# Hash attention and gated feed-forward: the normed rows of five half batches turned by DMA instead of TensorE

## The chip, the cores and the metric

The kernel runs on one core of one Trainium2 chip. The metric is the device time of one execution in microseconds; lower is better. Before the change three runs took 341.55, 342.83 and 345.98 us, so the median is 342.83 us.

## What is computed

Attention with hash buckets: a query sees only the keys whose six sign bits agree with its own. Its result, heads side by side, goes row by row through a root-mean-square norm and a gated feed-forward layer.

```python
# q, k, v: (4, 8, 768, 64); proj: (64, 6)
q_bits = einsum('bhsd,dk->bhsk', q, proj) > 0      # k_bits likewise
mask = bucket(q_bits)[:, :, :, None] == bucket(k_bits)[:, :, None, :]
scores = where(mask, q @ k.T / 8, -1e9)
attn = softmax(scores) @ v                         # denominator + 1e-9
x = attn.transpose(0, 2, 1, 3).reshape(3072, 512)
xn = x / sqrt(mean(x * x, -1) + 1e-6) * rms_g
g, val = xn @ w_gate, xn @ w_val                   # 512 -> 1536
out = (g * sigmoid(g) * val) @ w_out               # 1536 -> 512
```

## The kernel before

A batch has 768 tokens. The work is cut into eight half batches w = 0 to 7 of 384 tokens each; w // 2 is the batch. A token row of the feed-forward layer has 512 values, and a half batch has three chunks of 128 tokens.

**Slots.** One slot is a third of one head of one half batch: two score products (`scores`, L329) into a PSUM tile, one exponential over 128x768 (`probs`, L339). There are 192 slots (L34 to L36); from slot 48 on a half batch takes 24 slots. All other work is put into a plan by hand: `at(slot, function, ..., rank=)` (L556) hangs a step on a slot, and the loop at L679 writes the slot's steps out in order of rank: those with a rank below 3 ahead of the exponential, the others behind it, and steps of one rank in the order in which they were hung. The order in which instructions are written is the order in which each engine, and each engine's DMA queue, works them off. So a step that waits holds up what is written behind it on its engine.

**Stages of one half batch w.** `end` (L657) is three slots behind the last slot of a head.

- `av` (L341): the attention weights times v, at slots end-1 and end. Its keys' sums come from `v_sum` and `v_mean`.
- `attn_out` (L355), every second head, at slot end: VectorE adds the constant part (L366) and takes reciprocals (L371); GpSimd multiplies into `x` (L375) and squares (L387).
- `sumsq` (L390), six slots later: VectorE adds the squares of two heads up.
- `norm` (L396): VectorE adds the four parts (L398); GpSimd computes `ms` and, as a power of -0.5, `rstd` (L400, L404).
- `scale_x` (L406), one per chunk: VectorE multiplies the rows by `rstd`, from fp32 to fp16, into `xn` (L409).
- `turn_x` (L411), one per chunk: TensorE transposes the chunk's four 128x128 blocks into one PSUM bank (L416), and VectorE takes the bank into `xnT`, times the gain by column, `gcol` (L417). The feed-forward products need the 512 features on the partitions, and `xnT` has them so: four groups of 128 features by 384 tokens.
- `gate` and `value` (L422, L433), for twelve groups of 128 hidden features over 16 slots, beginning at slot s0 = 24 w + 48: each four matmuls over `xnT`. ScalarE takes a tanh of the gate (L430); VectorE forms `a` and `ht` from it (L440, L441).
- `project` (L447), nine steps over slots s0+16 to s0+24: TensorE multiplies with `wo`, ScalarE copies the bank to `ysb` (L459, two buffers), and SyncE stores it (L461).

For w >= 2 the last head's `end` is 24 w + 26, so the feed-forward part of a half batch runs while the scores of the half batch after next are worked on: gate stage w over slots s0 to s0+16, then its projection stage.

**Banks.** `gps` (L71) has three PSUM banks, in turn for gates, values, turns, projections, hash products and sums; the next user of a bank waits until the one before has been read.

**Loads and hash.** For batches 2 and 3 and the second half of batch 1, `load_blocks` (L115) fetches q and k of a pair of heads in four DMAs each, `load_rows` (L107) v in one, all on SyncE's queue, into a ring of ten raw tiles. VectorE turns q and k in 32x32 blocks (`turn_dve`, L193), GpSimd casts them to fp16 (`cast_pool`, L201), `hash_pairs` (L274) computes the sign bits, and eight (or four) DMAs on SyncE's queue (L288) put them beside q and k. `v_prep` and `v_sum` (L293, L297) cast v and add its six blocks up on GpSimd. The table `work` (L616) holds, per pair of heads (batch, pair), the slots of the k, q and v loads, of the turns, of the casts, and of the hash.

Weights are loaded early by GpSimd's queue. The rows' gain is loaded as `gcol`, 128 partitions by four columns (L551).

```python
    for w in range(8):
        for h in range(H):
            end = LAST[w, h] + 3
```

Of the kernel before, what the change touches and what calls it, by code (L numbers as in the profile page):

```python
# [8 lines left out]
FP32 = mybir.dt.float32  # L9
FP16 = mybir.dt.float16  # L10
AF = mybir.ActivationFunctionType
ALU = mybir.AluOpType
# [5 lines left out]
D = 64  # L18
DMODEL = H * D
# [7 lines left out]
KBIT = -32.0  # L27
ESCALE = 1.0 / 8.0
C0 = 1.0e-9

# [11 lines left out]
def kernel(  # L44
# [12 lines left out]
    nc = tc.nc  # L57
    PSUM = bass.MemoryType.PSUM

    const = ctx.enter_context(tc.tile_pool(name="const", bufs=1))  # L60
# [7 lines left out]
    spool = ctx.enter_context(tc.tile_pool(name="spool", bufs=2))  # L68
# [13 lines left out]
    scl = const.tile([128, 1], FP32, name="scl")  # L82
    mhalf = const.tile([128, 3], FP32, name="mhalf")
    gcol = const.tile([128, 4], FP32, name="gcol")
    wg = const.tile([128, 4, DFF], FP16, name="wg")
    wv = const.tile([128, 4, DFF], FP16, name="wv")
    wo = const.tile([128, NF, DMODEL], FP16, name="wo")
    vls = [const.tile([128, H, 6, 66], FP16, name=f"vl{i}") for i in range(2)]
    vsum = [const.tile([128, H, 66], FP16, name=f"vsum{i}") for i in range(2)]
    cvb = [const.tile([128, H, 66], FP32, name=f"cvb{i}") for i in range(2)]  # L90

    def bank(name, shape=None, dt=FP32):
        return gps.tile(shape or [128, 512], dt, name=name, tag="g")
# [203 lines left out]
    def v_sum(b, hp):  # L297
        vn = raw[b, hp, "v"]
        hs = slice(2 * hp, 2 * hp + 2)
        a = spool.tile([128, 2, 3, D], FP32, name="vadd")  # L300
        nc.gpsimd.tensor_add(a, vn[:, :, 0:3], vn[:, :, 3:6])
        nc.gpsimd.tensor_add(a[:, :, 0], a[:, :, 0], a[:, :, 1])
        nc.gpsimd.tensor_add(vsum[b % 2][:, hs, 0:64], a[:, :, 0], a[:, :, 2])

    def v_mean(b, hp, n, parts=(None,)):
        hs = slice(2 * hp, 2 * hp + n)
        ps = bank("m_ps", [128, n, 65])
        for i, jt in enumerate(parts):
# [3 lines left out]
            )  # L312
        nc.vector.tensor_scalar_mul(cvb[b % 2][:, hs, 0:65], ps, C0 / S)  # L313


    sps, psb, ot = {}, {}, {}
    x, ssp, xn, xnT, ht = {}, {}, {}, {}, {}
# [76 lines left out]
    rstds = {}  # L394
# [11 lines left out]
    def scale_x(w, c):  # L406
        if w not in xn:
            xn[w] = npool.tile([128, 3, DMODEL], FP16, name="xn")
        nc.vector.tensor_scalar_mul(xn[w][:, c, :], x[w][:, c, :], rstds[w][:, c : c + 1])  # L409

    def turn_x(w, c):  # L411
        if w not in xnT:
            xnT[w] = npool.tile([128, 4, HALF], FP16, name="xnT", bufs=2)
        ps = bank("x_ps", [128, 4, 128], FP16)
        for kt in range(4):
            nc.tensor.transpose(ps[:, kt, :], xn[w][:, c, kt * 128 : (kt + 1) * 128], ident16)  # L416
        nc.vector.tensor_mul(  # L417
            xnT[w][:, :, c * 128 : (c + 1) * 128], ps,
            gcol.unsqueeze(2).to_broadcast([128, 4, 128]),
        )  # L420
# [87 lines left out]
    def load_wo(f0, f1):  # L508
        nc.gpsimd.dma_start(
            out=wo[:, f0:f1, :],  # L510
            in_=moe_w_out[f0 * 128 : f1 * 128, :].rearrange("(k p) n -> p k n", p=128),
        )

    def columns_of_proj():
# [41 lines left out]
    def at(s, f, *a, rank=3):  # L556
        plan[s].append((rank, len(plan[s]), lambda: f(*a)))
# [36 lines left out]
    for i, (t, src) in enumerate(((wg, moe_w_gate), (wv, moe_w_val))):  # L594
        at(2 + 4 * i, load_w, t, src, 0, 768)
        at(12 + 5 * i, load_w, t, src, 768, 1536)
        at(33 + 6 * i, load_wo, 6 * i, 6 * i + 6)
# [15 lines left out]
    def in_row(loads, s, hash_slot=None):  # L613
        return loads, range(s, s + 8), (s + 4, s + 8, s + 9), hash_slot
# [2 lines left out]
        (1, 2): ((21, 23, 30), (36, 37, 40, 40, 48, 49, 50, 51), (42, 52, 46), 53),  # L617
        (1, 3): in_row((42, 44, 47), 52, 61),
        (2, 0): in_row((54, 56, 59), 61), (2, 1): in_row((64, 67, 70), 71, 80),
        (2, 2): in_row((73, 76, 79), 81), (2, 3): in_row((82, 85, 88), 91, 100),  # L620
        (3, 0): in_row((94, 98, 102), 106), (3, 1): in_row((104, 108, 112), 116, 125),
        (3, 2): in_row((116, 120, 124), 126), (3, 3): in_row((126, 130, 134), 136, 145),
    }
    for (b, hp), (loads, turns, cast_slots, sh) in work.items():
        for which, s in zip("kqv", loads):
            at(s, load_rows if which == "v" else load_blocks, nc.sync, b, hp, which)
        for i, s in enumerate(turns):
            at(s, turn_dve, b, hp, "kq"[i // 4], i % 4, rank=5)
        for which, s in zip("kq", cast_slots):
            at(s, cast_pool, b, hp, which)  # L630
        if sh:
            at(sh, hash_pairs, b, (hp,) if b == 1 else (hp - 1, hp))
        at(cast_slots[2], v_prep, b, hp)
        at(cast_slots[2], v_sum, b, hp)
        if hp % 2:
            at(64 if b == 1 else 48 * b - 4 + 4 * hp, v_mean, b, hp - 1, 4)
    for hp in range(2):
        at(52 + 4 * hp, v_mean, 1, hp, 2, range(6))

    gts, sqs = {}, {}  # L640

# [13 lines left out]
# [3 lines that stand above are left out]
            at(end - 1, av, w, h, 0, 9)  # L658
            at(end, av, w, h, 9, 18)
            if h % 2:  # L660
                at(end, o_step, w, h // 2, rank=4.5)
                if (w, h) != (0, 7):
                    at(end + 6, s_step, w, h // 2, rank=5)
        at(end + (1 if w == 0 else 9), norm, w, rank=5)
        for c in range(3):
            at(end + (3 if w == 0 else 14 + c), scale_x, w, c, rank=5)
            at(end + (7 + c if w == 0 else 17 + 2 * c), turn_x, w, c, rank=1)
        s0 = 24 * w + 48
        seen = set()
        for ft in range(NF):  # L670
            for f, s in ((g_step, s0 + 16 * ft // NF), (v_step, s0 + (32 * ft + 16) // (2 * NF))):
                at(s, f, w, ft, rank=4 if s in seen else 2)
                seen.add(s)
        for i in range(9 if w < 7 else 6):
            c, j = divmod(i, 3)
            at(s0 + 16 + i, project, w, c, 4 * j, 4 * j + 4, rank=1 if i == 8 else 3)


    for s in range(NS + 48):  # L679
# [3 lines left out]
        n = sum(r < 3 for r, _, _ in todo) if s < NS - 1 else 0  # L683
# [54 lines left out]
```

## Time and profile before

| | before |
|---|---|
| median of three runs | 342.83 us (341.55 to 345.98) |
| the profiled execution | 341.45 us, of which the span 339.7 us |
| granted TensorE clock | 1.00 of full speed |
| TensorE busy | 329.8 us (97% of the span) |
| VectorE busy | 238.5 us (70%) |
| ScalarE busy | 210.0 us (62%) |
| GpSimd busy | 151.5 us (45%) |
| 16 DMA engines, packets of SyncE's queue | 31.5% of their span |
| transposes on TensorE into `x_ps` (L416) | 96, of 218 ns each in flight |
| their evictions on VectorE (L417) | 24, 684 ns each |
| scales on VectorE (L409) | 24, 651 ns each |

The span is the time from the profiled execution's first instruction to its last, and what lies around it is the rest of the device time. In the views below, PE is TensorE's matmuls, PEld its weight loads, DVE VectorE, ACT ScalarE, POOL GpSimd and SPq SyncE's queue. A line names the source line (L438), the tile written and the tiles read. TensorE's matmuls overlap, so the duration of one is longer than what it adds to the stream: the chain of waits shows the latter. The row of digits has 40 equal slices of the span, each digit the busy share in tenths.

### The profile page before, as it was taken

How to read it: one execution, taken by the hardware profiler on the slowest of the kernel's cores; microseconds unless marked ns; L12 is line 12 of the kernel's file. 1: busy time of each engine (PE TensorE's matmuls, PEld its weight loads, DVE VectorE, ACT ScalarE, POOL GpSimd, SP SyncE). 2: the span in 40 equal slices, each digit the busy share in tenths (PEclk: the TensorE clock that was granted, in tenths of full speed). 3: DMA queues.
4: the chain of work that ended last, by engine and by line, in shares of the span. 5: the costliest groups of instructions: out<-in, count | busy, mean ns of one | idle time of the engine just before them, and what ended most of it. 6: DMA issues, size and time to landing. Idle time of an engine off the chain costs nothing.

```text
span 339.7 us, 7799 instructions
## 1 busy us (share of the span) xinstructions
PE 329.8 (97%) x3004; PEld 201.5 (59%) x3004; DVE 238.5 (70%) x529; ACT 210.0 (62%) x328; POOL 151.5 (45%) x224
## 2 busy tenths in 40 slices
PE   8899989999999999999999999999999999999995
PEld 7566656564566565566565665566566665555553
DVE  4769798888758895778668886767436653883860
ACT  3789987666566675657666675567666774322321
POOL 4879878437366576335737385503111311110000
PEclk9999999999999999999999999999999999999999
DMA  7999999744646074418243341100010001002002
GB/s 205 351 220 256 196 186 156 140 66 91 117 131 128 17 139 103 91 28 175 64 101 74 59 98 63 39 13 2 31 64 0 3 23 69 5 0 93 3 0 93
DMA packets 80052, 31.36 MB, mean 92 GB/s; under 512 B 65144, under 2 KB 77072, under 8 KB 80016
## 3 DMA queue, kind: packets, MB, share of 16 engines
q1 hardware_dynamic: 76080, 26.09, 31.5%
q0 software_dynamic: 3712, 4.72, 8.6%
q8 instruction: 23, 0.38, 0.5%
q14 instruction: 13, 0.11, 0.1%
q10 hardware_dynamic: 224, 0.07, 0.1%
HBM read 28.32 MB, written 6.29 MB: 102 GB/s over the span
## 4 chain that ended last, share of the span: by engine, by line
PE 88%; DVE 9%; issue 1%; ACT 1%; DVEq 0%; ACTq 0%
PE v_ps L438 18%; PE y_ps L452 18%; PE g_ps L428 18%; PE s_ps L329 16%; PE o_ps L351 9%; PE d_ps L209 5%; PE x_ps L416 1%; PE t_ps L169 1%; DVE otmp L366 1%; PE z_ps L322 1%; PE y_ps L695 1%; DVE xn L409 1%; DVE ssp L391 1%; PE m_ps L310 1%; DVE QK L270 1%
## 5 line engine op out<-in xcount | busy, mean ns | idle before, releaser
L339 ACT ACTIVATE psb<-s_ps 128x768 f16<-128x768 f32 x192 | 150.8, 809 | 29.1 <-PE s_ps L329 27.9
L329 PE MATMUL s_ps<-QK 76*128 76x384 f16 x384 | 93.5, 325 | 1.3 <-ACT psb L339 0.7
L430 ACT ACTIVATE t<-g_ps 128x384 f32<-128x384 f32 x96 | 47.1, 490 | 62.4 <-PE g_ps L428 62.1
L438 PE MATMUL v_ps<-xnT,wv 128*128 128x384 f16 x384 | 78.0, 325 | 0.9 <-DVE cvb L313 0.5
L428 PE MATMUL g_ps<-xnT,wg 128*128 128x384 f16 x384 | 78.0, 325 | 0.4 <-DVE xnT L417 0.4
L440 DVE SCALAR_TENSOR_TENSOR a<-t,g_ps 128x384 f32<-128x384 f32 x96 | 52.6, 548 | 28.2 <-ACT t L430 26.3
L452 PE MATMUL y_ps<-wo,ht 128*128 128x512 f16 x276 | 69.2, 378 | 0.5 <-DVE a L440 0.5
L375 POOL TENSOR_TENSOR x<-otmp,rcp 128x384 f32<-128x384 f32 x31 | 25.8, 831 | 95.8 <-DVE rcp L371 95.5
L351 PEld LDWEIGHTS <-psb 128*128 128x128 f16 x1152 | 51.5, 97 | 25.0 <-issue 7.5
L441 DVE SCALAR_TENSOR_TENSOR ht<-a,v_ps 128x384 f16<-128x384 f32 x96 | 53.2, 554 | 11.5 <-PE v_ps L438 2.3
L351 PE MATMUL o_ps<-vl,psb 128*128 128x65 f16 x1152 | 56.7, 193 | 0.4 <-DVE otmp L366 0.2
L438 PEld LDWEIGHTS <-wv 128*128 128x128 f16 x384 | 36.3, 97 | 25.3 <-issue 1.7
L428 PEld LDWEIGHTS <-wg 128*128 128x128 f16 x384 | 35.9, 97 | 24.3 <-issue 0.6
L329 PEld LDWEIGHTS <-QK 76*128 76x128 f16 x384 | 31.6, 98 | 16.4 <-issue 3.6
L452 PEld LDWEIGHTS <-ht 128*128 128x128 f16 x276 | 25.8, 97 | 24.3 <-issue 0.6
L459 ACT COPY ysb<-y_ps 128x512 f32<-128x512 f32 x23 | 13.5, 586 | 25.4 <-PE y_ps L452 22.6
L417 DVE TENSOR_TENSOR xnT<-x_ps,gcol 128x512 f16<-128x512 f16 x24 | 16.3, 684 | 15.9 <-PE x_ps L416 15.9
L387 POOL TENSOR_TENSOR sq<-x 128x384 f32<-128x384 f32 x31 | 25.6, 825 | 2.5
L366 DVE TENSOR_TENSOR otmp<-o_ps,cvb 128x390 f32<-128x390 f32 x32 | 17.8, 557 | 10.3 <-PE o_ps L351 10.3
L201 POOL CAST QK<-kT 64x768 f16<-64x768 f32 x20 | 16.7, 834 | 13.5 <-DVE kT L193 6.5
L216 DVE TENSOR_SCALAR bits<-d_ps,thr,scl 128x384 f16<-128x384 f32 (+1 forms) x20 | 13.3, 675 | 11.4 <-PE d_ps L209 10.1
L201 POOL CAST QK<-qT 64x768 f16<-64x768 f32 x20 | 16.7, 835 | 9.2 <-DVE qT L193 8.6
(77 smaller groups left out, 285.9 us busy)
## 6 DMA issues: line engine op xcount, KB each, us to landing
vL<-in_v_dram SPq DMA_DIRECT2D x16, 384.0 KB
out_dram<-ysb SPq DMA_DIRECT2D x23, 256.0 KB
kL<-in_k_dram SPq DMA_DIRECT2D x40, 96.0 KB
qL<-in_q_dram SPq DMA_DIRECT2D x40, 96.0 KB
kL<-in_k_dram SPq DMA_DIRECT2D x5, 384.0 KB
qL<-in_q_dram SPq DMA_DIRECT2D x5, 384.0 KB
wg<-in_moe_w_gate_dram POOLq DMA_DIRECT2D x2, 768.0 KB, 8.0
wv<-in_moe_w_val_dram POOLq DMA_DIRECT2D x2, 768.0 KB, 10.8
```

The lines of the kernel that those rows point to most:

```text
L201: nc.gpsimd.tensor_copy(QK[b, hp][0:64, hh, o : o + S], T0[b, hp, which][64 * hh : 64 * hh + 64, :])
L329: nc.tensor.matmul(ps[:, j, 0:HALF], k_cols(w // 2, h, 2 * p + j), q_cols(w, h), start=True, stop=True,)
L339: nc.scalar.activation(psb[w, h][:, p], sps.pop(g)[:, :, 0:HALF], AF.Exp, scale=ESCALE,)
L351: nc.tensor.matmul(o[:, c, hh, 0:65], psb[w, h][:, jt // 2, jt % 2, 128 * c : 128 * c + 128], vls[b % 2][:, h, v_chunk(b, h, jt), 0:65], s ...
L375: eng.tensor_mul(xd.rearrange("p c (h d) -> p c h d", h=2), tmp[:, :, :, 0:64], r.to_broadcast([128, 3, 2, 64]),)
L387: nc.gpsimd.tensor_mul(sq, xd, xd)
L428: nc.tensor.matmul(g, wg[:, kt, fs], xnT[w][:, kt], start=(kt == 0), stop=(kt == 3))
L430: nc.scalar.activation(t, g, AF.Tanh, scale=0.5)
L438: nc.tensor.matmul(vv, wv[:, kt, fs], xnT[w][:, kt], start=(kt == 0), stop=(kt == 3))
L440: nc.vector.scalar_tensor_tensor(out=a, in0=t, scalar=1.0, in1=g, op0=ALU.add, op1=ALU.mult)
L441: nc.vector.scalar_tensor_tensor(out=ht[w][:, ft], in0=a, scalar=0.5, in1=vv, op0=ALU.mult, op1=ALU.mult)
L452: nc.tensor.matmul(y, ht[w][:, ft, c * 128 : (c + 1) * 128], wo[:, ft, :], start=(ft == 0), stop=(ft == NF - 1),)
```

## The change

For half batches 2 to 6 (`BY_DMA`), `turn_x` issues four transposing DMAs per chunk on SyncE's queue, from `xn` straight into `xnT`, in place of four TensorE transposes and one eviction. The gain, which the eviction multiplied in by column, is now multiplied in by `scale_x`: a scalar_tensor_tensor of the rows, `rstd`, and a new tile `grow`, in which the gain stands along the row on every partition (128x512 fp32, loaded by one DMA on SyncE's queue at slot 63).

The row sums of these half batches stand four slots behind `attn_out` where they stood six (for each pair of heads), the norm at end+5 where it stood at end+9, the scales at end+7, 8 and 9 where they stood at end+14, 15 and 16, and the turns in the same slots as the scales, behind them, where they stood at end+17, 19 and 21. Half batches 0, 1 and 7 keep theirs.

Loads of three pairs of heads stand elsewhere in the plan: k and q of (2, 3) at slots 80 and 81 for 82 and 85; of (3, 1) at 103 and 104 for 104 and 108; of (3, 3) at 126 and 127 for 126 and 130, and the v of (3, 3) at 138 for 134.

`v_sum` adds in another order, over two tiles' width where it had three, with one buffer for two.

```diff
+BY_DMA = (2, 3, 4, 5, 6)
...
+    grow = const.tile([128, DMODEL], FP32, name="grow")
...
-        a = spool.tile([128, 2, 3, D], FP32, name="vadd")
-        nc.gpsimd.tensor_add(a, vn[:, :, 0:3], vn[:, :, 3:6])
-        nc.gpsimd.tensor_add(a[:, :, 0], a[:, :, 0], a[:, :, 1])
-        nc.gpsimd.tensor_add(vsum[b % 2][:, hs, 0:64], a[:, :, 0], a[:, :, 2])
+        a = spool.tile([128, 2, 2, D], FP32, name="vadd", bufs=1)
+        nc.gpsimd.tensor_add(a, vn[:, :, 0:2], vn[:, :, 2:4])
+        nc.gpsimd.tensor_add(a, a, vn[:, :, 4:6])
+        nc.gpsimd.tensor_add(vsum[b % 2][:, hs, 0:64], a[:, :, 0], a[:, :, 1])
...
-        nc.vector.tensor_scalar_mul(xn[w][:, c, :], x[w][:, c, :], rstds[w][:, c : c + 1])
+        if w in BY_DMA:
+            nc.vector.scalar_tensor_tensor(
+                out=xn[w][:, c, :], in0=x[w][:, c, :], scalar=rstds[w][:, c : c + 1],
+                in1=grow, op0=ALU.mult, op1=ALU.mult,
+            )
+        else:
+            nc.vector.tensor_scalar_mul(xn[w][:, c, :], x[w][:, c, :], rstds[w][:, c : c + 1])
...
+        if w in BY_DMA:
+            for kt in range(4):
+                nc.sync.dma_start(
+                    out=xnT[w][:, kt, c * 128 : (c + 1) * 128],
+                    in_=xn[w][:, c, kt * 128 : (kt + 1) * 128], transpose=True,
+                )
+            return
...
+    def load_grow():
+        nc.sync.dma_start(
+            out=grow, in_=moe_rms_g.rearrange("(o n) -> o n", o=1).to_broadcast([128, DMODEL])
+        )
...
-        (2, 2): in_row((73, 76, 79), 81), (2, 3): in_row((82, 85, 88), 91, 100),
-        (3, 0): in_row((94, 98, 102), 106), (3, 1): in_row((104, 108, 112), 116, 125),
-        (3, 2): in_row((116, 120, 124), 126), (3, 3): in_row((126, 130, 134), 136, 145),
+        (2, 2): in_row((73, 76, 79), 81), (2, 3): in_row((80, 81, 88), 91, 100),
+        (3, 0): in_row((94, 98, 102), 106), (3, 1): in_row((103, 104, 112), 116, 125),
+        (3, 2): in_row((116, 120, 124), 126), (3, 3): in_row((126, 127, 138), 136, 145),
...
+    at(63, load_grow)
...
-                    at(end + 6, s_step, w, h // 2, rank=5)
-        at(end + (1 if w == 0 else 9), norm, w, rank=5)
+                    at(end + (4 if w in BY_DMA else 6), s_step, w, h // 2, rank=5)
+        at(end + (1 if w == 0 else 5 if w in BY_DMA else 9), norm, w, rank=5)
         for c in range(3):
-            at(end + (3 if w == 0 else 14 + c), scale_x, w, c, rank=5)
-            at(end + (7 + c if w == 0 else 17 + 2 * c), turn_x, w, c, rank=1)
+            scale, turn, rank = (3, 7 + c, 1) if w == 0 else (14 + c, 17 + 2 * c, 1)
+            if w in BY_DMA:
+                scale, turn, rank = 7 + c, 7 + c, 6
+            at(end + scale, scale_x, w, c, rank=5)
+            at(end + turn, turn_x, w, c, rank=rank)
```

## The prediction, made before the result was known

> **What bounds the kernel now.** I read the page's first two parts, then the chain of waits, then the chain in order of time around one gate, then the sync queue and VectorE over the same stretch.
>
> ```profile
> PE 329.8 (97%) x3004; PEld 201.5 (59%) x3004; DVE 238.5 (70%) x529; ACT 210.0 (62%) x328; POOL 151.5 (45%) x224
> PE   8899989999999999999999999999999999999995
> PE 88%; DVE 9%; issue 1%; ACT 1%; DVEq 0%; ACTq 0%
> ```
>
> TensorE is the bound: of 339.7 us it is idle for 9.9, and the windows put 4.7 of that ahead of 58 us and 4.3 behind 287 us. From 58 to 287 us only 0.97 us are idle. So what leaves TensorE's stream in this middle is gained in full, unless something else then comes late, and no more than about 1 us of idle time is there to be won besides.
>
> Chain in order of time, around the first gate of half batch 2 (w=2, slot 96):
>
> ```profile
> 126.84 0.23 PE x_ps L416 x4
> 130.01 0.23 PE x_ps L416 x4
> 132.90 0.23 PE x_ps L416 x4
> 134.60 0.86 PE y_ps L452 x4
> 135.46 0.65 PE g_ps L428 x4
> ```
>
> Each turn of one 128-token chunk costs TensorE 0.23 us, and the first gate begins at 135.46. The same chain has the gates of w=3 to 6 at 174.36, 212.44, 250.77 and 286.57: some 1.6 us a slot.
>
> SyncE's queue over the same stretch (start, duration, what; durations of a queue are issue with waits):
>
> ```profile
> 112.22 6.55 SPq L288 DMA_DIRECT2D QK<-bits  x8
> 118.87 2.70 SPq L121 DMA_DIRECT2D kL<-in_k_dram  x4
> 121.61 2.71 SPq L121 DMA_DIRECT2D qL<-in_q_dram  x4
> 124.37 0.64 SPq L111 DMA_DIRECT2D vL<-in_v_dram  x1
> 127.16 4.94 SPq L461 DMA_DIRECT2D out_dram<-ysb  x2
> ```
>
> SyncE works the bits, then k and q, without a pause. An issue costs it 0.34 (out) to 0.71 us (bits, median of x28; 0.64 for k and q).
>
> VectorE in the gate stage before (w=1), where the scales are moved to:
>
> ```profile
> 116.86 0.55 DVE L441 SCALAR_TENSOR_TENSOR ht<-a,v_ps 128x384 f16<-128x384 f32 x1
> 117.33 0.52 DVE L193 STREAM_TRANSPOSE kT<-kL 128x192 f32<-128x192 f32 x1
> 117.70 0.15 DVE L398 TENSOR_REDUCE ss<-ssp 128x3 f32<-128x12 f32 x1
> 118.14 0.56 DVE L440 SCALAR_TENSOR_TENSOR a<-t,g_ps 128x384 f32<-128x384 f32 x1 [0.29 <-ACT t L430]
> ```
>
> From 110.87 to 124.4 this 0.29 us is VectorE's only marked idle time: it is full there, though its share of the span is 70%.
>
> **What goes.** 60 transposes (5 half batches x 3 chunks x 4) leave TensorE: 15 groups x 0.227 us = **-3.4 us**, all in the middle. With them go 15 evictions (L417, 0.684 us, 10.3 us of VectorE) and 15 turns of a PSUM bank; these lie in the projection stage, where VectorE waits for TensorE anyway (161.6 to 174.4: 8.5 of 12.8 us busy): 0.
>
> **What comes on SyncE.** 12 transposing DMAs of 128x128 per half batch. No row of the trace has one; T is the time that each takes in a row on the queue. Eight DMAs can be in flight (each waits for the eighth before it), so a landing slower than 8T would set T instead. Work it out for w=2. Its rows are scaled by about 117, but in SyncE's order the turns stand behind bits, k and q of head pairs (2,2) and (2,3): they begin at 121.61 + 2.71 = 124.32. Landing: the cast at 120.05 that waited for bits was let go 1.29 us after their last issue ended (118.76). TensorE reaches the gate at 135.46 - 0.68 (its own three groups) = 134.78. What is left for 12 T is 134.78 - 124.32 - 1.29 = 9.17 us: **T up to 0.76 us is hidden**. The same sum for w=3 (q ends at 158.28, gate 174.36, 0.68 off): 14.1 us. For w=4 (197.71, 212.44): 12.8 us. For w=5 and 6 SyncE is idle and the scales set the start (about 229.1 and 265.5): 18.3 and 16.4 us.
> The price of T is then the sum of what 12 T exceeds these five by. Ends: 0.34 us, the cheapest issue of the queue, price 0; and 1.43, twice its dearest, since a transposing issue has to cut its block up and no row shows into how much: 17.2 us each, 8.0 + 3.1 + 4.4 + 0 + 0.8 = **+16.2**. I take 0.71, the bits' row, the only one from SBUF to SBUF like these: price 0, but 0.6 us are in hand at w=2.
> The Trainium skill, "VectorE: DVE Perf Modes", section "The three transpose paths", gives 1309 ns for one 128x128 transpose by DMA, and speaks for TensorE where PSUM will do; by that as T, the price would be 6.5 + 1.6 + 3.0 = 11.1 us and the kernel slower. "Advanced Engine Details and Errata", section "X-Bar Transpose (TRN2)", says that such DMAs are as fast as ordinary ones, by which the price is 0. No trace here shows which.
>
> **What stands behind the turns on SyncE.** The v load of (2,3) goes from 124.37 to 124.32 + 8.57 = 132.9; its cast begins near 144, so it is covered until T is about 1.3. The first output store of w=1 goes from 127.16 to 133.6. ysb has two buffers, so ScalarE's third copy (135.54 before) waits until that store has landed, at about 135.6: 0.7 us late at most. TensorE is let off, as ScalarE idled 1.74 us there: 0, at most +0.7. The loads "moved ahead" (k, q of (2,3), (3,1), (3,3)) start no sooner: before, too, SyncE reached them straight after the bits. Their order among the loads is kept. The gain row's load (256 KB, one more issue at slot 63, like an output store's 0.34) has 45 us until its use: 0. GpSimd queues no new DMA.
>
> **What comes on VectorE.** 15 scales become scalar_tensor_tensor of two fp32 SBUF operands, 128x512. Bounds: L441 at 554 ns for 384 elements, at the same slope (128 columns in 0.14 us more) 0.69 us; and the one product of two SBUF operands on VectorE (L375, 843 ns for 384), 1.12 us. I take 0.8, nearer to L441, which is the same instruction. They stand at slots 81 to 83 (and 105, 129) of the full stretch, behind that slot's `a` and `ht`. Added: 3 x 0.8 = 2.4 us. The last row sum (0.52) and the norm (0.15) leave the stretch forwards: net 1.7 us late. What waits: three PSUM banks turn, and the gate at 120.74 needs the bank that the ht of 118.80 freed at 119.35, the value product at 119.81 the one that `a` freed at 118.70; so 1.1 us of lateness is free. The rest stalls TensorE: 0.6 us for each of w=2, 3 and 4; none for w=5 and 6, where VectorE has no k and q turns left (225.5 to 238: 9.2 of 12.5 us). **+1.9**, ends 0 and 3 x (3.4 - 0.7 - 1.1) = +4.8.
> The scales also wait for rstd two slots (3.2 us) behind the norm: ms and pow take 1.2 us on GpSimd, with at most a cast pair (1.7) ahead: 0. The row sums two slots sooner (four behind o_step, 6.4 us): the rows show x and sq done within 2 us behind rcp: 0, at most 0.5.
> v_sum adds 256 + 256 + 128 elements for 384 + 128 + 128: the same 640, by the slope of L301 and L302 the same 1.93 us: 0.
>
> **The sum.** -3.4 + 1.9 + 0 = -1.5 us. The profiled execution took 341.45 us (span 339.7), 1.4 below the median 342.83 of three: the profiled one would become 340.0, the median **341.3**.
>
> **Rivals.**
> (1) Slow turns: T above 0.76, SyncE's queue in place of TensorE's turns. Place: the first gate of w=2, then of w=4 and 3. Against it is that no issue in this trace needs more than 0.71 without a wait; for it, that w=2 has only 0.6 us in hand and that a transpose has more to cut up than any DMA here. From T = 0.89 the loss of w=2 alone (12 T - 9.17 = 1.5) eats more than the gain; from 1.24 on (36 T - 36.1 = 6.9 + 1.5) it is over 2% slower. At T = 1.43: 341.3 + 16.2 = 357.5 us. The 1309 ns of the Trainium skill (same page and section as above) would give 341.3 + 11.1 = 352.4; no run here shows it.
> (2) VectorE becomes the bound of the gate stage: 1.12 us a scale, -3.4 + 4.8: 344.2. For it: the stretch without idle time; against: at w=3 it idles about 1 us between 150 and 157 us, where lateness is caught up.
> (3) All hidden: VectorE's lateness is caught up and T is small: 342.83 - 3.4 = 339.4. For it: 1.1 us slack at each bank; against: no idle time until the projection stage.
>
> **How the numbers follow.** Forecast 0.37 (339.9 to 343), slow turns 0.42 (0.36 of it beyond 2%), VectorE 0.11, all hidden 0.10. The likeliest is 341.3, its own range 339.9 to 343. The range of eight in ten leaves out the far end of T and the best case's lower fringe: 339.2 to 355. Two per cent (6.9 us) is about what a measurement of this kernel can tell from no change; 3.4 + 1 us is all that TensorE can give back, so faster by over 2% is 0.02, within 0.62, slower 0.36.
>
> **What would show it.** Right: no x_ps group between 96 and 287 us; twelve issues of about 0.7 us behind q of (2,3), over before the gate; no releaser "DMA xnT" ahead of g_ps; short waits of TensorE for `a` or `ht` in the gate stages of w=1 to 3. Wrong: g_ps or its weight loads waiting for xnT, longest at w=2; SyncE issuing turns past 134 us; ScalarE's ysb waiting for output stores. The forecast falls if T is over 0.9, or if a turn in flight holds up plain DMAs.

## The result, and the profile after

The changed kernel takes 364.63 us (median of 6 runs, 362.26 to 367.92) against 342.71 us (6 runs, 341.55 to 345.98) for the kernel before: ratio 1.0626, 95% interval 1.0564 to 1.0688. The ratios leave out runs that stood in a slower state (here the one of 367.92 us), and need not equal the quotient of two medians. The changed kernel is slower by 6.3%, where 341.3 us and "within 2%" were forecast, and it lies above the range. Its profiled execution took 362.26 us, its span is 360.5 us against 339.7.

The page, after (parts 1, 2 and 4):

```profile
PE 336.2 (93%) x2944; PEld 200.4 (56%) x2944; DVE 231.6 (64%) x514; ACT 209.6 (58%) x328; POOL 152.7 (42%) x224
PE   8999989999999994999969999699999999999995
PEclk9999999999999997799998999989999999999999
PE 72%; DVE 15%; SPq 5%; DMA 3%; issue 2%; ACT 2%; DVEq 0%; ACTq 0%
```

Two things are to be read here. TensorE's row, a line of nines before, has three holes (slices 16, 21 and 26: from 135, 180 and 225 us on, 9 us each), and the granted clock dips under the first and in the slice behind each. And TensorE has 60 instructions fewer but is busy 6.4 us longer, though 3.4 us of transposes are gone: some 9.8 us of busy time are new, and the same matmuls at a lower clock are what the profile offers for them (a gate matmul takes 0.32 us in some rows below, 0.48 to 0.50 in others). In the chain SyncE's queue (SPq) and DMA, absent before, hold 8% between them.

When does each half batch's first gate matmul begin? From the timelines of TensorE, the period from one half batch to the next, in us:

| from w to w | 0-1 | 1-2 | 2-3 | 3-4 | 4-5 | 5-6 | 6-7 |
|---|---|---|---|---|---|---|---|
| before | 40.84 | 37.91 | 38.90 | 38.08 | 38.33 | 35.80 | 25.41 |
| after | 40.47 | 40.52 | 46.52 | 44.35 | 43.32 | 35.81 | 25.42 |
| after less before | -0.4 | +2.6 | +7.6 | +6.3 | +5.0 | 0 | 0 |

All of the loss comes from the gates of w=2, 3 and 4 and what follows each. At w=5 and 6, where SyncE has no loads left, the same turns lose nothing; but the 0.68 us of transposes that leave TensorE ahead of w=6 are not won there either (35.81 against 35.80). SyncE's queue ahead of the first gate of w=2 (start, duration, what):

```profile
111.31 6.57 SPq L292 DMA_DIRECT2D QK<-bits  x8
117.99 2.69 SPq L125 DMA_DIRECT2D kL<-in_k_dram  x4
120.73 2.71 SPq L125 DMA_DIRECT2D qL<-in_q_dram  x4
123.55 16.09 SPq L426 DMA_TRANSPOSE xnT<-xn  x12
139.69 0.58 SPq L115 DMA_DIRECT2D vL<-in_v_dram  x1
140.37 0.89 SPq L478 DMA_DIRECT2D out_dram<-ysb  x2
```

The turns begin where the prediction had them, right behind q, but twelve of them take 16.09 us and not 8.5, and the output stores stand behind them until 140.37. What this does to TensorE, and then to ScalarE (timelines of both, idle time and releaser in brackets):

```profile
133.71 1.03 PE L469 MATMUL y_ps<-wo,ht 128*128 128x512 f16 x4
137.00 0.32 PE L445 MATMUL g_ps<-xnT,wg 128*128 128x384 f16 x1 [2.26 <-DMA xnT<-xn]
138.31 0.32 PE L445 MATMUL g_ps<-xnT,wg 128*128 128x384 f16 x1 [0.99 <-DMA xnT<-xn]
139.57 0.48 PE L445 MATMUL g_ps<-xnT,wg 128*128 128x384 f16 x1 [0.94 <-DMA xnT<-xn]
140.82 0.50 PE L445 MATMUL g_ps<-xnT,wg 128*128 128x384 f16 x1 [0.77 <-DMA xnT<-xn]
...
144.85 1.44 PE L445 MATMUL g_ps<-xnT,wg 128*128 128x384 f16 x4 [0.71 <-ACT ysb L476]
```

```profile
144.21 0.58 ACT L476 COPY ysb<-y_ps 128x512 f32<-128x512 f32 x1 [10.91 <-PE s_ps L333]
...
189.13 0.58 ACT L476 COPY ysb<-y_ps 128x512 f32<-128x512 f32 x1 [6.88 <-DMA out_dram<-ysb]
```

The four gate matmuls of w=2 each wait for the turn of their own 128 features of the last chunk, about 1.26 us apart: TensorE runs at SyncE's pace. Then comes a second wait. ScalarE's third ysb copy stands still until 144.21. The view puts that down to s_ps, which had long been done; with two ysb buffers the copy needs the store issued at 140.37 to land, and at w=3 the same wait carries the store's name. The gate behind it is held in turn. The chain in order of time shows both landings:

```profile
137.14 1.23 SPq L426
138.37 0.04 issue
138.41 2.36 DMA xnT<-xn
...
185.12 3.91 DMA out_dram<-ysb
```

One turn holds SyncE 1.23 us and the next follows 0.04 us later: a pitch of 1.27 us. The last one, issued from 138.41 to 139.64, lands 2.36 us after its issue has begun and 1.13 us after it has ended. That is far below 8 T = 10.2 us, so it isn't the landing that sets T. At w=3 the chain runs through a store whose issue began at 185.12, behind the turns and a v load, and which landed 3.91 us later.

Windows of 2 us around w=2 (columns: window and us, busy us of PE, PEld, DVE, ACT, POOL with counts, granted clock, DMA share, GB/s):

```profile
136.00:138.00 2.00, 0.32 (x1) 0.10 (x1) 0.00 (x0) 0.00 (x0) 0.00 (x0) 1.00 0.11 20
138.00:140.00 2.00, 0.75 (x2) 0.10 (x1) 0.00 (x0) 0.00 (x0) 0.00 (x0) 0.80 0.16 33
140.00:142.00 2.00, 0.77 (x3) 0.28 (x3) 0.43 (x1) 0.00 (x0) 0.00 (x0) 0.50 0.51 126
146.00:148.00 2.00, 2.00 (x15) 1.23 (x14) 2.00 (x5) 1.68 (x3) 0.00 (x0) 0.50 1.00 227
148.00:150.00 2.00, 2.00 (x17) 1.24 (x16) 1.26 (x5) 0.33 (x1) 0.00 (x0) 0.64 0.89 132
```

TensorE is nearly idle from 134.7 us on. The clock falls to 0.50 at about 139.2 (a mean of 0.80 from 138 to 140 is 1.2 us at 1.00 and 0.8 at 0.50), and by the same working it is back at 1.00 at about 149.4, some 4.6 us after TensorE's stream runs without a gap again (from 144.85). And while the turns run alone (136 to 140) the DMA engines are busy 0.11 to 0.16 of the time: it doesn't look as if moving the data took the 1.27 us; the first two experiments test it.

### The profile page after: what moved, and what is told of

It reads as the page before. It is cut to its first block, busy times and chain, and to the rows that moved or that the text cites. A ratio compares the mean times of both kernels' runs of the same rounds, so it can differ in the third digit from the quotient of the medians.

```text
span 360.5 us, 7752 instructions
## 1 busy us (share of the span) xinstructions
PE 336.2 (93%) x2944; PEld 200.4 (56%) x2944; DVE 231.6 (64%) x514; ACT 209.6 (58%) x328; POOL 152.7 (42%) x224
## 4 chain that ended last, share of the span: by engine, by line
PE 72%; DVE 15%; SPq 5%; DMA 3%; issue 2%; ACT 2%; DVEq 0%; ACTq 0%
PE v_ps L455 16%; PE g_ps L445 14%; PE y_ps L469 14%; PE s_ps L333 12%; PE o_ps L355 8%; SPq L426 5%; PE d_ps L213 4%; DVE otmp L370 2%; DVE a L457 2%; DMA out_dram<-ysb 2%; DVE xn L414 2%; DVE ht L458 1%; PE t_ps L173 1%; PE z_ps L326 1%; PE y_ps L722 1%
## 5 line engine op out<-in xcount | busy, mean ns | idle before, releaser
L333 PE MATMUL s_ps<-QK 76*128 76x384 f16 x384 | 94.8, 329 | 1.2 <-ACT psb L343 0.7
L445 PE MATMUL g_ps<-xnT,wg 128*128 128x384 f16 x384 | 80.5, 329 | 12.8 <-DMA xnT<-xn 6.8
L455 PE MATMUL v_ps<-xnT,wv 128*128 128x384 f16 x384 | 80.3, 332 | 2.9 <-DVE a L457 1.5
L355 PEld LDWEIGHTS <-psb 128*128 128x128 f16 x1152 | 52.7, 99 | 26.3 <-issue 9.1
L355 PE MATMUL o_ps<-vl,psb 128*128 128x65 f16 x1152 | 57.9, 195 | 0.4 <-DVE otmp L370 0.4
L333 PEld LDWEIGHTS <-QK 76*128 76x128 f16 x384 | 31.9, 98 | 16.4 <-issue 3.9
L391 POOL TENSOR_TENSOR sq<-x 128x384 f32<-128x384 f32 x31 | 27.3, 879 | 2.4
L220 DVE TENSOR_SCALAR bits<-d_ps,thr,scl 128x384 f16<-128x384 f32 (+1 forms) x20 | 13.3, 675 | 10.7 <-PE d_ps L213 9.5
L197 DVE STREAM_TRANSPOSE qT<-qL 128x192 f32<-128x192 f32 x40 | 19.4, 518 | 0.0
```

The source lines that it names most:

```text
L333: nc.tensor.matmul(ps[:, j, 0:HALF], k_cols(w // 2, h, 2 * p + j), q_cols(w, h), start=True, stop=True,)
L355: nc.tensor.matmul(o[:, c, hh, 0:65], psb[w, h][:, jt // 2, jt % 2, 128 * c : 128 * c + 128], vls[b % 2][:, h, v_chunk(b, h, jt), 0:65], s ...
L391: nc.gpsimd.tensor_mul(sq, xd, xd)
L445: nc.tensor.matmul(g, wg[:, kt, fs], xnT[w][:, kt], start=(kt == 0), stop=(kt == 3))
L455: nc.tensor.matmul(vv, wv[:, kt, fs], xnT[w][:, kt], start=(kt == 0), stop=(kt == 3))
```

## The experiments

The theory that came out of the two traces: a turn costs SyncE 1.27 us for the issue, whatever it moves; twelve of them are too many ahead of the gates of w=2 to 4; and the stores behind them make a second wait. All ratios below are against the kernel before, run on the same chip.

**One issue for a chunk in place of four.** The same data, in a quarter of the issues.

```diff
-            for kt in range(4):
-                nc.sync.dma_start(
-                    out=xnT[w][:, kt, c * 128 : (c + 1) * 128],
-                    in_=xn[w][:, c, kt * 128 : (kt + 1) * 128], transpose=True,
-                )
+            nc.sync.dma_start(
+                out=xnT[w][:, :, c * 128 : (c + 1) * 128], in_=xn[w][:, c, :], transpose=True,
+            )
```

> The changed kernel with one transposing DMA of 128x512 per chunk in place of four of 128x128: the same blocks in 3 issues per half batch instead of 12. Theory A (an issue costs a fixed time on SyncE): the pitch stays near 1.3 us, 3 issues take 4 us, the turns of all five half batches are over before their gates, no wait for xnT or for output stores is left, and the kernel comes out near 340 to 342 us. Theory B (SyncE's time goes with the blocks cut): an issue takes about 4 x 1.2 = 4.9 us, 14.7 us per half batch, and the time stays within 2 us of the changed kernel's 364.6.

Measured: 339.97 us, ratio 0.9955 (0.9923 to 0.9987). The turns' line in the view by tile, of the changed kernel and then of this one (count, ns as minimum/median/maximum, first and last start):

```profile
L426 SPq DMA_TRANSPOSE xnT<-xn x60: 1097/1230/2322, 123.6 to 302.6; - x60
```

```profile
L425 SPq DMA_TRANSPOSE xnT<-xn x15: 1188/1220/2715, 123.2 to 269.0; - x15
```

Four times the block in the same 1.22 us. SyncE's queue shows what that leaves of the turns of w=2 and of w=3:

```profile
123.21 5.42 SPq L425 DMA_TRANSPOSE xnT<-xn  x3
...
157.76 3.88 SPq L425 DMA_TRANSPOSE xnT<-xn  x3
```

They are over at 128.63, no gate waits for them, the clock is 0.999 over the span, and the whole loss of 22 us is gone. The gain row, the loads' new order, the new `v_sum` and the early scales are all still in this run, so none of them carries the loss. The price goes by the issue.

**Half blocks: twice the issues, the same data.** The opposite test.

```diff
-            for kt in range(4):
+            for i in range(8):
+                kt, t0_ = i // 2, 64 * (i % 2)
                 nc.sync.dma_start(
-                    out=xnT[w][:, kt, c * 128 : (c + 1) * 128],
-                    in_=xn[w][:, c, kt * 128 : (kt + 1) * 128], transpose=True,
+                    out=xnT[w][:, kt, c * 128 + t0_ : c * 128 + t0_ + 64],
+                    in_=xn[w][t0_ : t0_ + 64, c, kt * 128 : (kt + 1) * 128], transpose=True,
                 )
```

> As the changed kernel, with each transposing DMA cut in two (64 x 128 in place of 128 x 128), so 24 issues in a half batch and the same bytes. Theory (the price is that of an issue, whatever its size): each issue still takes 1.15 to 1.25 us, the 24 take some 30 us, the turns end some 14 us later in each of the five half batches; the gates of w = 2 to 4 then wait some 14 us longer, those of w = 5 and 6 begin to wait: the time is 410 to 440 us. Rival (the price is that of the block moved): 0.6 us for each issue, 24 in 15 us, the time stays at 364 to 366 us.

Measured: 439.95 us, ratio 1.2837 (1.2723 to 1.295). By tile, on SyncE's queue at w=2, and TensorE's longest kind of wait (us in total, times, longest):

```profile
L427 SPq DMA_TRANSPOSE xnT<-xn x120: 1102/1226/2428, 124.3 to 380.7; - x120
```

```profile
124.26 31.53 SPq L427 DMA_TRANSPOSE xnT<-xn  x24
```

```profile
PE g_ps L446 <- DMA xnT<-xn: 74.8, 20, 13.9
```

Half the block, the same 1.23 us an issue; 24 take 31.5 us. With the run before this settles it: 64x128, 128x128 and 128x512 cost SyncE the same.

**Turns by DMA at w=5 and 6 alone**, where SyncE is idle.

```diff
-BY_DMA = (2, 3, 4, 5, 6)
+BY_DMA = (5, 6)
```

> The changed kernel with half batches 5 and 6 alone turned by DMA, where SyncE has no loads left. Theory (SyncE's queue is what is late): 12 issues of 1.27 us (15.2) and a landing of 2.4 fit into the 18.3 and 16.4 us that I worked out, so no gate waits; with 6 groups of 0.23 us gone from TensorE the kernel comes out at 341 to 343, against 342.7 before. Rival (a turn in flight or the early scales on VectorE cost by themselves): each of the two half batches loses some us, 346 or more.

Measured: 341.16 us, ratio 0.9995 (0.9966 to 1.0024). SyncE's queue:

```profile
229.36 15.52 SPq L426 DMA_TRANSPOSE xnT<-xn  x12
244.97 5.65 SPq L478 DMA_DIRECT2D out_dram<-ysb  x3
266.08 15.73 SPq L426 DMA_TRANSPOSE xnT<-xn  x12
```

The turns are as long as in the changed kernel, 15.5 to 15.7 us, but over at 244.9 and 281.8. The gates of w=5 and 6 begin 4.6 and 3.2 us behind each; no wait for xnT appears in the trace, and the stores that now stand behind the turns hold nobody there. (The landing of 2.4 us in the expectation counts from the issue's beginning; from its end it is 1.13.) So a slow turn by itself costs next to nothing; it must meet a gate or a store that somebody waits for. The 1.4 us of TensorE's work that six chunks' turns take (6 x 0.227) are too little to show in this interval; in the profiled execution the period 4-5 is 0.66 us shorter than before's and 5-6 only 0.23, and what takes the rest of the second isn't shown.

**The change without its DMAs:** sums, norm and scales early, with the gain in the scale, but TensorE turns as before at the old slots.

```diff
-        if w in BY_DMA:
-            for kt in range(4):
-                nc.sync.dma_start(
...
-            return
...
+        if w in BY_DMA:
+            nc.vector.tensor_copy(xnT[w][:, :, c * 128 : (c + 1) * 128], ps)
+            return
...
-                scale, turn, rank = 7 + c, 7 + c, 6
+                scale = 7 + c
```

> The changed kernel's early row sums, norms and scales with the gain (half batches 2 to 6), but the turns done by TensorE at their old slots, evicted by a plain copy; no transposing DMA at all. Theory (the turns on SyncE's queue are the cause): at most the 1.9 us that I gave VectorE, so 342.5 to 345. Rival (VectorE full in the gate stage is the cause): most of the 22 us loss stays, 355 or more.

Measured: 343.13 us, ratio 1.0055 (1.0034 to 1.0076), so +1.8 us for what VectorE is asked to do earlier; the prediction had +1.9. In size this agrees; by place it does so in part, as the prediction had 0.6 us for each of w=2, 3 and 4: the periods 1-2 and 3-4 are 0.84 and 1.2 us longer than before's, the first 0.4 shorter, the others equal. A scale's duration, in the view by tile of the changed kernel:

```profile
L414 DVE SCALAR_TENSOR_TENSOR xn<-x,rstd,grow x15: 666/745/1240, 113.5 to 291.0; 128x512 f16<-128x512 f32 x15
```

**The output stores of w=1 to 3 off SyncE's queue,** first on ScalarE's:

```diff
-            nc.sync.dma_start(out=rows[:, out_chunk(w, c), :], in_=ysb)
+            eng = nc.scalar if 1 <= w <= 3 else nc.sync
+            eng.dma_start(out=rows[:, out_chunk(w, c), :], in_=ysb)
```

> The changed kernel with the output stores of half batches 1 to 3 on ScalarE's queue, so that they no longer stand behind the turns on SyncE's. Theory (a second loss sits behind the turns: ScalarE's third copy waits for a store that SyncE has not issued, some 3 us at the gate of half batch 2, 4 at 3 and 4 at 4, with the clock's fall after it): 8 to 13 us are won, 352 to 357. Rival (the wait for xnT is all of the loss, the stores land in its shadow): within 2 us of 364.6.

Measured: 381.38 us, ratio 1.118 (1.1131 to 1.123): slower by another 17 us. The chain of this run at w=2:

```profile
130.30 0.59 ACT ysb L476
...
130.91 2.18 DMA out_dram<-ysb
...
133.11 1.10 SPq L426
```

The first turn is issued at 123.00; the second waits for a store on ScalarE's queue, which is issued at 130.91 and lands 2.18 us later, so it starts at 133.11. SyncE's queue stood 8.9 us for that store, and the twelve turns take 23.97 us. It looks as if the eight places in flight that the prediction counted were shared by both queues, but no run shows that this is why; in any case the edit put a store in front of a turn. The run tells nothing of the question that it was made for.

Then on GpSimd's queue (`nc.gpsimd` in place of `nc.scalar`), where no turn waits for a store:

> The changed kernel (12 issues per half batch) with the output stores of half batches 1 to 3 on GpSimd's queue, which shares no completion lane with SyncE's. It repeats the question of the stores on ScalarE's queue, where the turns on SyncE came to wait for the stores' lanes. Theory (a second loss sits behind the turns: ScalarE's third copy waits for a store that SyncE cannot issue until the turns and the v load are through): TensorE resumes right behind the landing of the turns, 3.4 us earlier at half batch 2, 3.5 at 3, 2.7 at 4, together with some of the clock's fall 9 to 14 us: 350 to 356. Rival (the stores' wait lies in the shadow of the wait for xnT): within 2 us of 364.6.

Measured: 350.17 us, ratio 1.0249 (1.0202 to 1.0297), against 1.0626 for the changed kernel, with the turns as long as there (15.77 us at w=2). 3.8 of the 6.3 points were thus the stores behind the turns, with what the clock made of that wait. TensorE's waits, of the changed kernel and of this run:

```profile
PE g_ps L445 <- DMA xnT<-xn: 6.8, 7, 2.3
PE g_ps L445 <- ACT ysb L476: 5.6, 3, 2.9
```

```profile
PE g_ps L445 <- DMA xnT<-xn: 5.8, 8, 2.4
```

The wait for ysb has gone, the wait for the turns is left.

**Is the lower clock a loss of its own?** 107 idle matmuls ahead of the first gate of w=2 keep TensorE busy while the turns go on, first with the stores on SyncE's queue.

```diff
+        if (w, ft) == (2, 0):
+            idle(g[:, 0:128], 107)
```

> The changed kernel with 107 idle products of 128x128 (they write the gate's bank, which the gate then overwrites) ahead of the first gate of half batch 2, where TensorE has 6 us to wait. Theory (part of the loss is the granted clock, 0.50 from 139.4 to 149.2 us behind that wait): the clock stays at 1.00 there and 2 to 4 us are won, 360.5 to 362.5. Rival (the waits are all of the loss): 364.6, or more if the idle products outlast the wait.

Measured: 364.8 us, ratio 1.0688 (1.063 to 1.0746): nothing won. The clock stayed at 1.00 until 144 us, but the store that landed late came next (timeline of TensorE):

```profile
134.79 6.14 PE L326 MATMUL g_ps<-ones 128*128 128x128 f16 x107
140.77 1.11 PE L447 MATMUL g_ps<-xnT,wg 128*128 128x384 f16 x4
...
145.41 1.44 PE L457 MATMUL v_ps<-xnT,wv 128*128 128x384 f16 x4 [3.42 <-ACT ysb L478]
```

TensorE then stood for 3.4 us, and the clock fell all the same: 0.64 from 144 to 146, then 0.50 until 150. The run mixes both; it was made again with the stores on GpSimd's queue:

> As the run with the stores of w = 1 to 3 on GpSimd's queue (350.2 us), with 107 idle matmuls on TensorE ahead of the first gate of w = 2, which still waits for the turns. With the stores off SyncE's queue, nothing else should hold the stages of w = 2, so the granted clock is the only thing that the fill changes. Theory (the clock that falls after TensorE's idleness is a loss of its own): the clock stays near 1.00 between 136 and 148 us, where it was 0.50 to 0.65 for 8 us, the period from the first gate of w = 2 to that of w = 3 falls from 42.9 to about 41, and the time is 348 to 349 us. Rival (TensorE had waits in those 8 us anyway): the clock stays up, the time is 350 us.

Measured: 349.92 us, ratio 1.0209 (1.0154 to 1.0264). Windows of the run without the fill, and of this one:

```profile
138.00:140.00 2.00, 0.80 (x2) 0.20 (x2) 0.00 (x0) 0.00 (x0) 0.00 (x0) 0.65 0.46 152
142.00:144.00 2.00, 2.00 (x9) 0.92 (x8) 1.30 (x3) 1.19 (x2) 0.00 (x0) 0.50 1.00 245
```

```profile
138.00:140.00 2.00, 2.00 (x40) 2.00 (x38) 0.00 (x0) 0.00 (x0) 0.00 (x0) 1.00 0.52 157
142.00:144.00 2.00, 1.73 (x16) 1.01 (x14) 0.38 (x1) 0.50 (x2) 0.00 (x0) 1.00 0.43 85
```

The clock held. The first gate of w=2 itself begins later here (142.21 against 138.30), so the two periods around it are taken together: from the first gate of w=1 to that of w=3, 82.75 us passed against 83.55 without the fill, although the turns of w=2 took 16.71 us here against 15.77. So in these profiles the clock is worth 0.8 us at w=2 and, with the longer turns set off, perhaps 1.7. The times can't confirm it: 349.92 us is the rival's 350, and the two ratios' intervals overlap. (This run's profiled execution took 353.69 us; what it lost more came behind 220 us, outside the stretch that is read.) Over all three half batches only a bound can be read. The run with one issue for a chunk has as many matmuls as the changed kernel:

```profile
PE 326.9 (97%) x2944; PEld 198.1 (59%) x2944; DVE 230.3 (68%) x514; ACT 209.9 (62%) x328; POOL 153.0 (45%) x224
```

The changed kernel's TensorE is busy 9.3 us longer for them (336.2) and idle 13.6 us longer (24.3 against 10.7); that is the 22.9 us between the two spans. So slower matmuls are at most some 9 of the 22.9 us, and how much of these is the clock's stays open.

**One issue for a chunk, and VectorE's work back at its old slots:** since three turns take 4 to 6 us and not 16, nothing has to be early.

```diff
-                    at(end + (4 if w in BY_DMA else 6), s_step, w, h // 2, rank=5)
-        at(end + (1 if w == 0 else 5 if w in BY_DMA else 9), norm, w, rank=5)
+                    at(end + 6, s_step, w, h // 2, rank=5)
+        at(end + (1 if w == 0 else 9), norm, w, rank=5)
...
-                scale, turn, rank = 7 + c, 7 + c, 6
+                scale, turn, rank = 14 + c, 14 + c, 6
```

> One issue per chunk, and row sums, norm and scales back at their old slots (6, 9 and 14 to 16 behind), each turn right behind its scale. Theory (with 3 issues the turns need some 6 us and not 20, so the scales need not stand in VectorE's full stretch): the gate still does not wait, VectorE's lateness goes, and all of the 3.4 us of transposes is gained against the kernel before: ratio 0.989 to 0.992. Rival (the turns then land too late, or the loads behind them on SyncE do): ratio of the early version, 0.9955, or above.

Measured: 338.06 us, ratio 0.9884 (0.9843 to 0.9926). The periods 1-2 to 5-6 are each 0.66 to 1.2 us shorter than before's: three groups of 0.227 us, or a little more, so the ratio comes out just below the 0.989 expected. The periods 1-2 to 4-5 are 0.56 to 0.85 us shorter than in the early version. Then with w=1 and 7 as well (`BY_DMA = (1, 2, 3, 4, 5, 6, 7)`, and the gain row loaded at slot 46):

> As the kernel with one issue per chunk and late scales, and half batches 1 and 7 turned by DMA too (the gain row loaded at slot 46). Theory: two more half batches at 0.68 us of TensorE each, 4.8 us in all: ratio 0.985 to 0.988. Rival: in half batch 7 the slots are short (no scores are left) and in half batch 1 SyncE is busy with bits and loads, so that a gate waits there: ratio 0.99 or above.

Measured: 337.08 us, ratio 0.9879 (0.9833 to 0.9925). The interval can't part it from the run before, but its span is the shortest, 334.5 us against 336.4, and both are faster than the kernel before and the changed one.

More ysb buffers might have taken the stores' wait away in another manner; that wasn't tried.

## Why the prediction was wrong

- **The step that failed first is the size of T**: "I take 0.71, the bits' row, the only one from SBUF to SBUF like these: price 0". T is 1.27 us, inside the bounds of 0.34 and 1.43 but near the end that I didn't take. Alike in source and target was no reason to be alike in price. The prediction's own sums, at T = 1.27 (12 T = 15.24), give 6.1 us for w=2, 1.1 for w=3, 2.4 for w=4 and 0 for w=5 and 6: 341.3 + 9.6 = 350.9 us. The run that has the turns but not the stores behind them took 350.2. So the place (w=2 first) and the mechanism held, and the number put in was wrong; that the total agrees within 1 us is partly luck. Against the run with one issue for a chunk, the periods of the run without the stores are longer by 2.6 and 4.6 us around w=2 (7.2 together, the lower clock included), 0.7 at 3-4, 1.1 at 4-5 and 0.7 at 5-6, where the sums have 6.1, 1.1, 2.4 and 0. The bound of 1.24 us for a loss of over 2% was just passed.
- The Trainium skill, "VectorE: DVE Perf Modes", section "The three transpose paths", gives 1309 ns for a 128x128 transpose by DMA; the pitch of 1.27 us is 3% below it, and the estimate that the prediction worked out from it, 352.4, would have been nearer, though it still leaves out the stores. The Trainium skill's "Advanced Engine Details and Errata", section "X-Bar Transpose (TRN2)", has such DMAs as fast as ordinary ones; by the trace that doesn't hold for the time that an issue holds SyncE's queue, 1.23 us against 0.34 to 0.71.
- **The second step that failed is the stores**: "0, at most +0.7". It cost more than the turns did: the ratio falls from 1.0626 to 1.0249 without the stores behind the turns, and from there to 0.9955 with one issue for a chunk. It was worked out at T = 0.71, where the first store of w=1 goes at 133.6. At T = 1.27 it goes at 140.37 and lands near 144.2, 8.6 us behind the 135.6 of the prediction: 6.8 us for the later issue, and 1.8 because it took 3.8 us to land where the prediction had 2.0. The same comes at w=3 and w=4. Rival (1) priced the gates at a large T and left this term at its small-T value, so even the 16.2 us of its far end were less than the 23 us between the forecast and the time.
- **The clock** was in no term. The terms sum waits, as if TensorE went on afterwards as before; at w=2 it went on at half the clock for about 10 us. Slower matmuls are at most some 9 us of the loss, as worked out above.
- A sum that is off, without harm: the 18.3 and 16.4 us of room at w=5 and 6 don't follow from the starts and gates beside them, which give 250.77 - 0.68 - 229.1 - 1.29 = 19.7 and, in the same way, 19.1. Only the 0.8 us of w=6 at T = 1.43 hangs on it.
- Right: TensorE's -3.4 us (the run with late scales and cheap turns gains 3.1 us by its medians, 4.0 by its ratio); VectorE's +1.9 (1.8 measured, in two of the three places); the scale at 0.745 us, inside 0.69 to 1.12 and near the 0.8 taken; the landing, taken as 1.29 us from the end of the last issue and measured as 1.13; w=5 and 6 without a wait for a turn; the v load covered until T is about 1.3: TensorE's waits name no v load and no cast of it. The sum of the first two, -1.5 us, is what the run with one issue for a chunk measured: 0.9955 x 342.83 = 341.3.

## What to carry to other kernels

Price a DMA that no row shows by its issue on the queue and not by its bytes, and if many small ones can be one large one, that is the first thing to write: here it turned a loss of 6.3% into a gain of 0.5%, and of 1.2% with VectorE's work back at its old slots. When a rival changes one number, work every other term through again at that number, above all what stands behind the slow thing on its queue. And price a wait of TensorE of 3 us or more at somewhat more than its length: the clock fell behind such waits here, though what that cost could only be bounded.

## What the runs showed of the hardware

- A transposing DMA from SBUF to SBUF holds SyncE 1.22 to 1.23 us for 64x128, 128x128 and 128x512 fp16 alike, with 0.04 us between two; the plain DMAs of this queue hold it 0.34 to 0.71 us. While only turns run, the DMA engines are busy 0.11 to 0.16 of the time.
- A turn lands 2.36 us after its issue has begun (1.13 us after it has ended), an output store of 128x512 fp32 behind the turns 3.91 us after its issue has begun.
- The granted clock fell to 0.50 about 4.4 us after TensorE's stream ended at w=2 (134.74 to 139.2), with two short matmuls in between, and returned some 4.6 us after the stream ran without a gap again (144.85 to 149.4). Behind the idle matmuls, where nothing ran from 141.9 us on, it fell about 2.7 us later (0.64 over 144 to 146 us puts the fall at 144.6). The Trainium skill, "TensorE: Matmul & The Clock Gate", section "Why this matters for your kernels", warns of half the clock after a gap of about 3 us; the trace agrees with the fall, and shows that single matmuls of 0.32 us, 1.3 us apart, don't prevent it.
- In this program a DMA on ScalarE's queue held up one on SyncE's: SyncE's queue stood 8.9 us before a turn until a store had landed, 2.18 us of it from that store's issue on. With the stores on GpSimd's queue no turn waited for one.
